# Weights converted in pairs of tiles, and the second layer's loads issued a step sooner

## The chip, the cores and the metric

The kernel runs on one core of a Trainium2 chip. The metric is the device time of one execution in microseconds (us), the median of several runs. TensorE multiplies matrices, VectorE and ScalarE work element by element, GpSimd (POOL) does some of the same, and SyncE (SP) issues most transfers; each engine works through its own instructions in program order.

## The reference, cut to what matters

```
x = attention(q, k, v)          # 4 batches x 576 tokens, 8 heads of 64, linear attention with decay
h = x @ w_in                    # 2304 tokens x 512 -> 2048
x = (h * sigmoid(h)) @ w_out    # first layer, 2048 -> 512
h = x @ w_in2
return (relu(h) ** 2) @ w_out2  # second layer, the same sizes
```

q, k and v are float32, the weights float64. The kernel reads a weight as a 64-bit word and turns it into float32 on the chip by integer steps. A product of two matrices is then made of a high part (rounded to the matmul's own format) and a low part (the rest): each product is high x high, high x low and low x high.

## The kernel before, in words

**Weights.** A tile is 128 x 512 words of 64 bits. Converting one takes four steps, each on one engine. `conv_a` (L107) makes two words of it with two activations on ScalarE (L115, L116). `conv_b` (L122 to L125) joins them on VectorE: a shift (L122), an addition (L123) and the sign (L125). `conv_c` casts the result to the high part on ScalarE (L137), and `conv_d` takes the difference, the low part, on VectorE (L141). `conv_to` runs the steps for tile i, i-1 and i-2 side by side. Raw tiles come by SP (`load_w`, L101) into a pool of three buffers (tag "wr"), the joined words into one of five (tag "wt"). There are 32 tiles in the first layer: wi (first GEMM) and wo (second GEMM) of 16 filters of 128 columns each.

**Blocks.** The first 1280 tokens of the first layer run in three blocks of 512, 384 and 384 tokens. Block 0 is where the weights are converted: for each filter f, `gemm1` (12 matmuls) makes ph, `gate` makes silu(ph) on ScalarE (L650) with its high part gh (L652), VectorE makes gl (L653), and two filters later `gemm2` (12 matmuls) adds to acc. The main loop (L1171) has two half-steps for each filter, and in each it emits conversions, waiting gates (`flush`), `gemm2` and attention. Attention for later tokens runs between the GEMMs as `scores_step` and `values_step`: `scores` (L369, L373) needs the keys scaled by `prep_k` (half of them on ScalarE, L358) and one PSUM tile, which `values` of the unit before it has to leave first; that unit's last reader is the difference xl (L465) on VectorE. `cut_consts(2)` (L306 to L309) cuts the tables that `prep_k` uses from then on, once, in the second half-step of the first filter.

**Second layer.** During block 1, the half-products of the other 1024 tokens (`product_s`) and their second GEMM (`gemm2_s`), `pre_step` walks a table of steps for the second layer's 16 pairs of tiles: load (`pre_load`), convert (`conv_a`, `conv_b`, one tile in each of two steps), four differences on GpSimd (`pre_sums`), and a store to DRAM. Behind it the second layer's products (L907, L998) run from DRAM copies. Transfers on SP are issued in program order, and one that waits for its buffer holds those behind it.

Of the kernel before, what the change touches and what calls it, by code (L numbers as in the profile page):

```python
# [29 lines left out]
LAG = 2  # L30
W1_FIRST, W1_AHEAD = 4, 4
AHEAD = 256
HALF = (slice(0, 64), slice(64, 128))
RAW = 3
# [9 lines left out]
def kernel(  # L44
# [23 lines left out]
    rp = l0_ctx.enter_context(tc.tile_pool(name="rp", bufs=RAW))  # L68
# [16 lines left out]

    wt = {}
    raw_w = {}
    order = sorted(range(2 * KF), key=lambda i: (i // 2 + i % 2 * LAG, i % 2))

    def w_at(n):  # L90

        layer, i = divmod(n, 2 * KF)
        return (layer, *divmod(order[i], 2))
# [25 lines left out]
    def conv_b(n, parts=(0, 1)):  # L119
        t, lo, hi = conv[n]  # L120
        if 0 in parts:
            nc.vector.tensor_scalar(t, t, 3, None, op0=ALU.logical_shift_left)  # L122
            nc.vector.tensor_tensor(t, t, lo, op=ALU.add)  # L123
        if 1 in parts:
            nc.vector.scalar_tensor_tensor(  # L125
                t, hi, -(2**31), t, op0=ALU.bitwise_and, op1=ALU.bitwise_or
            )

    def w_part(n):
        layer, f, part = w_at(n)  # L130
        if (part, f) not in wt:
            wt[part, f] = wp.tile([128, 2, 512], F32R, tag="w", name=("wi", "wo")[part])
        return wt[part, f][:, 0], wt[part, f][:, 1]
# [8 lines left out]

# [15 lines left out]
    woD = dp.tile([KF, 128, 2, 512], F32, name="woD")  # L158

    def keep_w(n):  # L160
        layer, f, part = w_at(n)
# [33 lines left out]
    def pre_parts(n):  # L195
        ta, tb = (conv["p", n, e][0].bitcast(F32) for e in range(2))
# [22 lines left out]
    def pre_store(n):  # L219
# [3 lines left out]
        if part == 0:  # L223
            nc.sync.dma_start(out=w1c[p, :, 0:512], in_=conv["p", n, 0][0].bitcast(F32))
# [8 lines left out]
        for e in range(2):  # L233
            conv.pop(("p", n, e))
# [4 lines left out]
    def pre_step():  # L239
# [37 lines left out]
    cs = cp.tile([128, 8 + 4 + 512 + 256 + 16], F32, name="cs")  # L277
    dummy = cp.tile([128, 1], F32, name="dummy")
    Tkn, dec = cs[:, 0:8], cs[:, 8:12]
# [31 lines left out]
    ap_ctx = ExitStack()  # L311
    ap = ap_ctx.enter_context(tc.tile_pool(name="ap", bufs=4, side="right"))
# [62 lines left out]
    def mask(u):  # L375
        rf_t[u] = rf = ap.tile([128, 2, 4, L], F32, tag="rf", name="rf", bufs=2)
# [176 lines left out]
    def first_units():  # L553
# [61 lines left out]
        conv_n[0] = 5  # L615
        conv_to(0, 6)
# [8 lines left out]
    def gemm1(layer, j, f, c0=0, c1=None):  # L625
# [6 lines left out]
        wh, wl = wt[0, f][:, 0], wt[0, f][:, 1]  # L632
# [12 lines left out]
    def gate(layer, j, f, ph):  # L645
# [3 lines left out]
        s = rp.tile([128, 512], F32, tag="wt", name="sg", bufs=5)[:, 0:n]  # L649
# [5 lines left out]
    def gemm2(layer, j, f):  # L655
        n = BLOCKS[j]
        gh, gl = g_t.pop((layer, j, f))
        wh, wl = wt[1, f][:, 0], wt[1, f][:, 1]
# [91 lines left out]
    def ws_at(p, c):  # L750
        if c in (0, 1, 6):
            w, c0 = wt[0, 2 * p + c // 6], c % 2 + c // 6
        else:
            w, c0 = ts[p, c // 2 - 1], c % 2
        return w[:, :, c0 * 256 : c0 * 256 + 256]

    def product_s(p, i):
# [5 lines left out]
        for k in range(2):  # L763
            w0 = slice(k * 128, k * 128 + 128)
            pairs += [(w[:, 0, w0], x[:, 0, k]), (w[:, 0, w0], x[:, 1, k]), (w[:, 1, w0], x[:, 0, k])]
# [666 lines left out]
```

## Time and profile before

| | |
|---|---|
| median of 3 runs | 828.31 us (828.2 to 828.74) |
| the profiled execution | 828.86 us, of which the span from the first to the last instruction is 827.1 us |
| TensorE busy | 811.1 us, 98% of the span |
| VectorE, ScalarE, GpSimd busy | 548.2, 450.5 and 184.3 us |
| mean granted TensorE clock | 0.998 |

An engine's busy time counts its instructions from start to end; TensorE's matmuls overlap, so its busy share says only that it has no gaps. A wait is a stretch in which an engine stands idle, put down to the instruction that released it.

### The profile page before, as it was taken

The page shows a single profiled execution, that of the slowest core. Times are in us where ns is not written, and L with a number is a line of the kernel's source. Part 1 is how long each engine was busy: PE and PEld are TensorE (multiplying, and loading weights), DVE is VectorE, ACT ScalarE, POOL GpSimd, SP SyncE. Part 2 cuts the span into 40 slices and gives each one's busy share as a digit, 9 for nine tenths or more (in the row PEclk, how much of TensorE's full clock was granted, in tenths as well). Part 3 has the DMA queues.
Part 4 walks back from the last instruction along what each step waited for, and adds up shares of the span by engine and source line. Part 5 has one row for each costly group of instructions (what it writes and reads, how often), then busy time and mean ns, then how long its engine had stood idle before and what let it go on. Part 6 is the DMA issues. An engine that isn't in the chain of part 4 may idle for free. (4 is left out here: it accounts for less than half of the span.)

```text
span 827.1 us, 16194 instructions
## 1 busy us (share of the span) xinstructions
PE 811.1 (98%) x6410; PEld 750.1 (91%) x6410; DVE 548.2 (66%) x809; ACT 450.5 (54%) x858; POOL 184.3 (22%) x205
## 2 busy tenths in 40 slices
PE   7999999999999999999999999999999999999998
PEld 6887789999888998888887999999999999999998
DVE  5799995554444655666778566545665988777771
ACT  5777874464455455454445576745667645433330
POOL 3202012313545204223432212401345000000000
PEclk9999999999999999999999999999999999999999
DMA  9787874987534022698787375243387844444300
GB/s 352 244 260 208 275 270 156 332 318 287 192 130 155 1 83 84 211 317 308 240 285 255 113 243 180 99 160 135 125 322 239 322 153 143 136 137 136 113 26 26
DMA packets 71980, 160.70 MB, mean 194 GB/s; under 512 B 6112, under 2 KB 37344, under 8 KB 71904
## 3 DMA queue, kind: packets, MB, share of 16 engines
q1 hardware_dynamic: 67008, 150.23, 53.5%
q10 hardware_dynamic: 4896, 9.44, 3.0%
q8 instruction: 50, 0.82, 0.4%
q14 instruction: 26, 0.21, 0.1%
HBM read 104.07 MB, written 55.57 MB: 193 GB/s over the span
## 5 line engine op out<-in xcount | busy, mean ns | idle before, releaser
L83 PE MATMUL acc<-gh,wo 128*128 128x384 f32 (+1 forms) x384 | 114.7, 360 | 0.0
L83 PE MATMUL ph<-xh,wi 128*128 128x384 f32 (+2 forms) x400 | 114.3, 350 | 0.0
L998 PE MATMUL pa<-w2s,gl 128*128 128x256 f32 x864 | 108.1, 283 | 0.0
L907 PE MATMUL pa<-xa,w1s 128*128 128x384 f32 x576 | 106.1, 335 | 0.7 <-DVE c L925 0.7
L998 PEld LDWEIGHTS pa<-w2s,gl 128*128 128x128 f32 x864 | 105.7, 192 | 0.0
L907 PEld LDWEIGHTS pa<-xa,w1s 128*128 128x128 f32 x576 | 100.3, 188 | 1.2 <-DVE c L925 1.0
L83 PE MATMUL acc<-gsl,wo 128*128 128x512 f32 x384 | 88.0, 390 | 0.5 <-DVE gsl L698 0.5
L83 PEld LDWEIGHTS acc<-gsl,wo 128*128 128x128 f32 x384 | 71.9, 188 | 16.4 <-DVE gsl L698 0.9
L697 ACT CAST gl<-gr 128x1024 fp32r<-128x1024 f32 (+1 forms) x57 | 55.7, 1002 | 51.8 <-DVE gr L972 25.3
L998 PE MATMUL pb<-w2s,gl 128*128 128x256 f32 x648 | 82.0, 283 | 0.0
L907 PE MATMUL pb<-xa,w1s 128*128 128x384 f32 x432 | 81.1, 336 | 0.0
L998 PEld LDWEIGHTS pb<-w2s,gl 128*128 128x128 f32 x648 | 79.6, 192 | 0.0
L83 PEld LDWEIGHTS ph<-xh,wi 128*128 128x128 f32 x400 | 72.7, 188 | 5.4
L83 PEld LDWEIGHTS acc<-gh,wo 128*128 128x128 f32 x384 | 71.5, 190 | 6.1
L907 PEld LDWEIGHTS pb<-xa,w1s 128*128 128x128 f32 x432 | 75.5, 188 | 0.5 <-DVE u L919 0.5
L698 DVE TENSOR_TENSOR gl<-gr,gl 128x1024 fp32r<-128x1024 f32 (+1 forms) x55 | 64.5, 1180 | 8.0 <-ACT gl L697 8.0
L83 PE MATMUL ph<-xl,wi 128*128 128x384 f32 (+2 forms) x200 | 69.3, 346 | 0.0
L83 PE MATMUL acc<-gl,wo 128*128 128x384 f32 (+1 forms) x192 | 68.6, 357 | 0.0
L653 DVE TENSOR_TENSOR gl<-sg,gh 128x384 fp32r<-128x384 f32 (+1 forms) x48 | 30.8, 643 | 47.6 <-ACT gh L652 47.6
L115 ACT ACTIVATE t<-wr 128x512 f32<-128x512 f32 x64 | 43.1, 673 | 28.3 <-DMA wr<-w 24.5
L650 ACT ACTIVATE sg<-ph 128x384 f32<-128x384 f32 (+1 forms) x48 | 25.0, 522 | 56.7 <-PE ph L83 54.5
L123 DVE CUSTOM_DVE_ANT_0 t<-wr,t 128x1024 uint16<-128x1024 uint16 x64 | 46.8, 731 | 7.7
(144 smaller groups left out, 1338.0 us busy)
## 6 DMA issues: line engine op xcount, KB each, us to landing
wr<-w SPq DMA_DIRECT2D x64, 512.0 KB, 4.4
gD<-g SPq DMA_DIRECT2D x48, 384.0 KB, 2.7
gr<-gD SPq DMA_DIRECT2D x36, 512.0 KB, 4.8
raw<-att SPq DMA_DIRECT2D x32, 512.0 KB, 4.6
woD<-wo SPq DMA_DIRECT2D x16, 512.0 KB, 7.1
wo<-woD SPq DMA_DIRECT2D x16, 512.0 KB, 7.4
w2r<-w2c SPq DMA_DIRECT2D x14, 512.0 KB, 6.1
xq<-x SPq DMA_DIRECT2D x12, 384.0 KB, 5.9
```

Of the source, the lines that this page charges most:

```text
L83: mm(o, a, b, start=first and i == 0, stop=last and i == n - 1)
L115: nc.scalar.activation(t.bitcast(F32), hi.bitcast(F32), ACTF.Abs, scale=2.0**-112)
L123: nc.vector.tensor_tensor(t, t, lo, op=ALU.add)
L650: nc.scalar.activation(s, ph, ACTF.Silu)
L653: later.append(lambda: nc.vector.tensor_sub(gl, s, gh))
L697: nc.scalar.copy(dst[0], src)
L698: low.append(lambda: engine.tensor_sub(dst[1], src, dst[0]))
L907: mm(o, lhs, rhs, start=m == 0 and i in (0, 1, 4), stop=m == 5, skip_group_check=True)
L998: mm(o, lhs, rhs, start=first, stop=m == NP - 1 and q == 2, skip_group_check=True)
```

## The change

Six tiles of the first layer (`SINGLES`) are converted as before, from buffers of the weight pool. The other 26 go in 13 pairs: two neighbouring filters of wi or of wo. The shift, the cast and the difference of a pair are single instructions over 1024 columns; the words, the addition and the sign are one instruction per raw tile, or one for the pair where both tiles came by one load into a single 8 KB buffer (tag "r8": three pairs of wi and the last of wo). `conv_step` puts the steps of a pair into half-steps: the words of pair q (`pair_a`) and the addition and sign of pair q-1 in one, the cast of pair q-1, its difference (behind the gates) and the shift of pair q in the next. In the first two half-steps it also finishes tiles 4 and 5. In the second layer each pair is loaded by one transfer into the "r8" buffer, one step sooner than before, its words made in one step and joined in the next. Buffers are laid out anew: the tables move to attention's pool, the mask has one buffer, the gates' tile a tag of its own with two, and the temporaries of the last stage always come from their pool. The saved wo goes to DRAM by pair and part. `pre_step` runs from the thirteenth product on and once per filter in the second GEMM of the half-products.

```diff
-W1_FIRST, W1_AHEAD = 4, 4
+W1_FIRST, SINGLES = 4, 6
 AHEAD = 256
 HALF = (slice(0, 64), slice(64, 128))
-RAW = 3
 WARM = 5
 NP = KF // 2
 HB = 384
...
+    w_order = [divmod(i, 2) for i in order[:SINGLES]]
+    pairs = [(part, j + 2 - part) for j in range(NP) for part in range(2) if j + 2 - part < NP]
+    def tiles_of(part, j):
+        if (part, j) not in w_pair:
+            w_pair[part, j] = ab = [
+                wp.tile([128, 2, 512], F32R, tag="w", name=("wi", "wo")[part] + nm) for nm in "hl"
+            ]
+            for e in range(2):
+                wt[part, 2 * j + e] = (ab[0][:, e], ab[1][:, e])
+        return w_pair[part, j]
     def load_w(n):
-        layer, f, part = w_at(n)
-        if n < W1_FIRST:
+        if n < SINGLES:
+            f, part = w_order[n]
             r = wp.tile([128, 512], U64, tag="w", name="wr")
-        else:
-            r = rp.tile([128, 512], U64, tag="wr", name="wr")
-        nc.sync.dma_start(out=r, in_=(w1, w2)[layer][f, part])
-        raw_w[n] = r
+            nc.sync.dma_start(out=r, in_=w1[f, part])
+            raw_w[n] = r
+            return
+        part, j = pairs[n - SINGLES]
+        if (part == 0 and j % 2 == 0) or (part and j == NP - 1):
+            r = rp.tile([128, 1024], U64, tag="r8", name="wr", bufs=1)
+            src = w1[2 * j : 2 * j + 2, part].rearrange("f p n -> p f n")
+            nc.sync.dma_start(out=r.rearrange("p (f n) -> p f n", f=2), in_=src)
+            raw_w[n] = [r]
+        else:
+            raw_w[n] = [wp.tile([128, 512], U64, tag="w", name="wr") for _ in range(2)]
+            for e, r in enumerate(raw_w[n]):
+                nc.sync.dma_start(out=r, in_=w1[2 * j + e, part])
     conv = {}
     first = {}
-    def conv_a(n):
-        r = raw_w.pop(n).bitcast(I32).rearrange("p (n t) -> p n t", t=2)
-        lo, hi = r[:, :, 0], r[:, :, 1]
-        if n in range(W1_FIRST):
-            t = wp.tile([128, 512], I32, tag="w", name="t")
-            first[n] = t
-        else:
-            t = rp.tile([128, 512], I32, tag="wt", name="t", bufs=5)
+    def words(r):
+        r = r.bitcast(I32).rearrange("p (n t) -> p n t", t=2)
+        return r[:, :, 0], r[:, :, 1]
+    def to_words(t, lo, hi):
         nc.scalar.activation(t.bitcast(F32), hi.bitcast(F32), ACTF.Abs, scale=2.0**-112)
         nc.scalar.activation(lo, lo.bitcast(U32), ACTF.Copy, scale=2.0**-29)
+    def add_sign(t, hi):
+        nc.vector.scalar_tensor_tensor(t, hi, -(2**31), t, op0=ALU.bitwise_and, op1=ALU.bitwise_or)
+    def conv_a(n):
+        lo, hi = words(raw_w.pop(n))
+        t = first[n] = wp.tile([128, 512], I32, tag="w", name="t")
+        to_words(t, lo, hi)
         conv[n] = (t, lo, hi)
...
+    def pair_a(n):
+        part, j = pairs[n - SINGLES] if isinstance(n, int) else (0, 0)
+        pool, tag = (wp, "w") if part and j < NP - 2 else (rp, "wr")
+        t = pool.tile([128, 1024], I32, tag=tag, name="t")
+        pieces = []
+        raws = raw_w.pop(n)
+        for e, r in enumerate(raws):
+            cols = 1024 // len(raws)
+            pieces.append((t[:, e * cols : e * cols + cols], *words(r)))
+            to_words(*pieces[-1])
+        conv[n] = (t, pieces)
+    def pair_b(n, part):
+        t, pieces = conv[n]
+        if part == 0:
+            nc.vector.tensor_scalar(t, t, 3, None, op0=ALU.logical_shift_left)
+        for tp, lo, hi in pieces:
+            if part == 1:
+                nc.vector.tensor_tensor(tp, tp, lo, op=ALU.add)
+            elif part == 2:
+                add_sign(tp, hi)
+    def pair_c(n):
+        nc.scalar.copy(flat(tiles_of(*pairs[n - SINGLES])[0]), conv[n][0].bitcast(F32))
+    def pair_d(n):
+        a, b = tiles_of(*pairs[n - SINGLES])
+        nc.vector.tensor_sub(flat(b), conv.pop(n)[0].bitcast(F32), flat(a))
...
     def keep_w(n):
-        layer, f, part = w_at(n)
+        if n < SINGLES:
+            f, part = w_order[n]
+            dst, t = w1f[f // 2, :, f % 2], first.pop(n)
+        else:
+            part, j = pairs[n - SINGLES]
+            dst, t = w1f[j].rearrange("p e n -> p (e n)"), conv[n][0]
         if part == 0:
-            t = first.pop(n) if n in first else conv[n][0]
-            nc.sync.dma_start(out=w1f[f // 2, :, f % 2], in_=t.bitcast(F32))
-    n_loaded = [0]
-    load_end = [2 * KF]
-    conv_n = [0, 0]
-    def load_next():
-        if n_loaded[0] < load_end[0]:
-            load_w(n_loaded[0])
-            n_loaded[0] += 1
-    def conv_to(layer, n):
-        for i in range(conv_n[layer], min(n, 2 * KF + 2)):
-            conv_n[layer] += 1
-            for lag, stage in ((2, conv_c), (0, conv_a), (1, conv_b), (2, conv_d)):
-                if 0 <= i - lag < 2 * KF:
-                    stage(layer * 2 * KF + i - lag)
-                    if stage is conv_b and n_loaded[0] < i - lag + layer * 2 * KF + RAW + 1:
-                        load_next()
-                    if stage is conv_b:
-                        keep_w(i - lag)
+            nc.sync.dma_start(out=dst, in_=t.bitcast(F32))
+    def conv_step(n):
+        if n < 2:
+            if n == 0:
+                conv_b(5)
+                load_w(SINGLES + 1)
+            conv_c(4 + n)
+            conv_d(4 + n)
+            if n == 0:
+                keep_w(4)
+                return
+        q, odd = divmod(n - 1, 2)
+        q += SINGLES
+        first, end = SINGLES, SINGLES + len(pairs)
+        if odd:
+            if first < q <= end:
+                pair_c(q - 1)
+                behind.append(lambda: pair_d(q - 1))
+            if q < end:
+                pair_b(q, 0)
+            return
+        if q < end:
+            pair_a(q)
+        if q + 2 < end:
+            load_w(q + 2)
+        if first < q <= end:
+            pair_b(q - 1, 1)
+            pair_b(q - 1, 2)
+            keep_w(q - 1)
...
     def pre_load(n):
         part, p = divmod(n, NP)
-        for e in range(2):
-            r = rp.tile([128, 512], U64, tag="wr", name="wr")
-            nc.sync.dma_start(out=r, in_=w2[2 * p + e, part])
-            raw_w["p", n, e] = r
+        r = rp.tile([128, 1024], U64, tag="r8", name="wr", bufs=1)
+        src = w2[2 * p : 2 * p + 2, part].rearrange("f p n -> p f n")
+        nc.sync.dma_start(out=r.rearrange("p (f n) -> p f n", f=2), in_=src)
+        raw_w["p", n] = [r]
...
-            if k == 0:
+            if k == (-1 if n else 0):
                 pre_load(n)
             elif k == 2:
-                conv_a(("p", n, 0))
+                pass
             elif k == 3:
-                conv_b(("p", n, 0))
-                conv_a(("p", n, 1))
+                pair_a(("p", n))
             elif k == 4:
-                conv_b(("p", n, 1))
+                for part in range(3):
+                    pair_b(("p", n), part)
...
         conv_a(4)
-        conv_n[0] = 5
-        conv_to(0, 6)
+        conv_c(3)
+        conv_a(5)
+        conv_b(4)
+        conv_d(3)
...
-        s = rp.tile([128, 512], F32, tag="wt", name="sg", bufs=5)[:, 0:n]
+        s = rp.tile([128, 512], F32, tag="sg", name="sg", bufs=2)[:, 0:n]
...
-                    conv_to(0, 2 * f + half + 1 + W1_AHEAD)
+                    conv_step(2 * f + odd)
...
-        if n >= 16 and n % 2 == 0:
+        if n >= 12 and n % 2 == 0:
             pre_step()
...
-        for _ in range(1 + n % 2 * (n < KF)):
-            pre_step()
+        pre_step()
```

## Rows read from the trace of the kernel before

**Rows 1.** The page: busy time, and VectorE and the granted clock in 40 slices of the span.

```profile
PE 811.1 (98%) x6410; PEld 750.1 (91%) x6410; DVE 548.2 (66%) x809; ACT 450.5 (54%) x858; POOL 184.3 (22%) x205
...
DVE  5799995554444655666778566545665988777771
...
PEclk9999999999999999999999999999999999999999
```

**Rows 2.** Windows by stage: stretch, us, each engine's busy us, clock, DMA share, GB/s.

```profile
60.00:100.00 40.00, 37.58 (x332) 30.26 (x331) 37.77 (x65) 30.74 (x57) 4.23 (x5) 0.96 0.81 250
```

**Rows 3.** Waits of TensorE: us in total, times, longest.

```profile
PE P L369 <- DVE xl L465: 2.4, 2, 2.0
...
PE P L369 <- ACT raw L358: 1.4, 3, 0.7
```

**Rows 4.** Timeline of VectorE: start, us, line, operation; start-up and two tiles of block 0.

```profile
31.56 0.69 DVE L125 SCALAR_TENSOR_TENSOR t<-wr,t 128x512 int32<-128x512 int32 x1
...
81.45 0.42 DVE L122 TENSOR_SCALAR t<-t 128x512 int32<-128x512 int32 x1
81.99 0.69 DVE L123 CUSTOM_DVE_ANT_0 t<-wr,t 128x1024 uint16<-128x1024 uint16 x1
82.72 0.69 DVE L125 SCALAR_TENSOR_TENSOR t<-wr,t 128x512 int32<-128x512 int32 x1
83.33 0.69 DVE L141 TENSOR_TENSOR wi<-t,wi 128x512 fp32r<-128x512 f32 x1
83.93 0.42 DVE L122 TENSOR_SCALAR t<-t 128x512 int32<-128x512 int32 x1
...
87.01 0.42 DVE L122 TENSOR_SCALAR t<-t 128x512 int32<-128x512 int32 x1
```

**Rows 5.** Timeline of TensorE in block 0; in brackets the idle time before.

```profile
38.37 0.50 PE L83 MATMUL acc<-gh,wo 128*128 128x512 f32 x1
...
53.43 0.39 PE L83 MATMUL ph<-xh,wi 128*128 128x512 f32 x1
...
58.87 0.39 PE L83 MATMUL ph<-xh,wi 128*128 128x512 f32 x1
...
94.67 0.69 PE L369 MATMUL P<-raw 64*64 64x64 f32 x32 [2.03 <-DVE xl L465]
...
95.77 0.68 PE L83 MATMUL acc<-gh,wo 128*128 128x512 f32 x1
...
100.22 0.39 PE L83 MATMUL ph<-xh,wi 128*128 128x512 f32 x1
```

**Rows 6.** Windows behind the stop at 94.67; the clock stands behind GpSimd's busy time.

```profile
96.00:97.00 1.00, 1.00 (x3) 0.82 (x3) 1.00 (x3) 0.97 (x3) 0.00 (x0) 0.50 0.76 285
```

**Rows 7.** Timeline of TensorE in the second GEMM of the half-products.

```profile
441.11 5.05 PE L83 MATMUL acc<-gsl,wo 128*128 128x512 f32 x21 [0.47 <-DVE gsl L698]
```

**Rows 8.** Groups by shape: count, busy us, mean ns of one, idle before.

```profile
L698 DVE TENSOR_TENSOR gl<-gr,gl 128x1024 fp32r<-128x1024 f32 x51 | 61.9, 1219 | 8.0 <-ACT gl L697 8.0
L697 ACT CAST gl<-gr 128x1024 fp32r<-128x1024 f32 x51 | 52.3, 1048 | 51.8 <-DVE gr L972 25.3 <-PE pa L998 12.2 <-DVE gr L974 9.8
...
L697 ACT CAST gl<-gr 128x512 fp32r<-128x512 f32 x6 | 3.4, 615 | 0.0
...
L698 DVE TENSOR_TENSOR gl<-gr,gl 128x512 fp32r<-128x512 f32 x4 | 2.6, 685 | 0.0
```

**Rows 9.** Timeline of ScalarE at the start of block 0.

```profile
36.54 1.05 ACT L358 ACTIVATE raw<-raw,cs 128x64 f32<-128x64 f32 x4
37.50 0.60 ACT L137 CAST wi<-t 128x512 fp32r<-128x512 f32 x1
38.01 0.67 ACT L115 ACTIVATE t<-wr 128x512 f32<-128x512 f32 x1
38.58 0.66 ACT L116 ACTIVATE wr<-wr 128x512 int32<-128x512 uint32 x1
```

**Rows 10.** The page's transfers: count, size, median us from issue to landing.

```profile
wr<-w SPq DMA_DIRECT2D x64, 512.0 KB, 4.4
```

More of the change, by code (lines that the diff above doesn't have):

```diff
@@ L86 @@
     wt = {}
+    w_pair = {}
     raw_w = {}
     order = sorted(range(2 * KF), key=lambda i: (i // 2 + i % 2 * LAG, i % 2))
-    def w_at(n):
-        layer, i = divmod(n, 2 * KF)
-        return (layer, *divmod(order[i], 2))
+    w_order = [divmod(i, 2) for i in order[:SINGLES]]
[8 more added lines that the diff above has]
+        return w_pair[part, j]
@@ L124, in conv_b @@
         if 1 in parts:
-            nc.vector.scalar_tensor_tensor(
-                t, hi, -(2**31), t, op0=ALU.bitwise_and, op1=ALU.bitwise_or
-            )
+            add_sign(t, hi)
     def w_part(n):
-        layer, f, part = w_at(n)
-        if (part, f) not in wt:
-            wt[part, f] = wp.tile([128, 2, 512], F32R, tag="w", name=("wi", "wo")[part])
-        return wt[part, f][:, 0], wt[part, f][:, 1]
+        f, part = w_order[n]
+        tiles_of(part, f // 2)
+        return wt[part, f]
     def conv_c(n):
@@ L195, in pre_parts @@
     def pre_parts(n):
-        ta, tb = (conv["p", n, e][0].bitcast(F32) for e in range(2))
+        t = conv["p", n][0].bitcast(F32)
+        ta, tb = t[:, 0:512], t[:, 512:1024]
         b11, b12, b21, b22 = ta[:, 0:256], tb[:, 0:256], ta[:, 256:512], tb[:, 256:512]
@@ L232, in pre_store @@
             nc.sync.dma_start(out=w2c[6, :, cols], in_=b22)
-        for e in range(2):
-            conv.pop(("p", n, e))
+        conv.pop(("p", n))
     pre_at = [5 * n if n < 6 else 3 + 5 * n for n in range(2 * NP)]
@@ L275 @@
     FOUR = ((0, 0), (1, 1), (0, 1), (1, 0))
-    cs = cp.tile([128, 8 + 4 + 512 + 256 + 16], F32, name="cs")
     dummy = cp.tile([128, 1], F32, name="dummy")
+    ap_ctx = ExitStack()
+    ap = ap_ctx.enter_context(tc.tile_pool(name="ap", bufs=4, side="right"))
+    cs = ap.tile([128, 8 + 4 + 512 + 256 + 16], F32, tag="cs", name="cs", bufs=1)
     Tkn, dec = cs[:, 0:8], cs[:, 8:12]
@@ L375, in mask @@
     def mask(u):
-        rf_t[u] = rf = ap.tile([128, 2, 4, L], F32, tag="rf", name="rf", bufs=2)
+        rf_t[u] = rf = ap.tile([128, 2, 4, L], F32, tag="rf", name="rf", bufs=1)
         nc.vector.tensor_mul(rf, P_of[u][:, :, 0:256].rearrange("p e (a t) -> p e a t", a=4), Tm)
@@ L753, in ws_at @@
         else:
-            w, c0 = ts[p, c // 2 - 1], c % 2
-        return w[:, :, c0 * 256 : c0 * 256 + 256]
+            w, c0 = (ts[p, c // 2 - 1][:, e] for e in range(2)), c % 2
+        return [part[:, c0 * 256 : c0 * 256 + 256] for part in w]
     def product_s(p, i):
@@ L764, in product_s @@
             w0 = slice(k * 128, k * 128 + 128)
[L765 removed]
+            pairs += [(w[0][:, w0], x[:, 0, k]), (w[0][:, w0], x[:, 1, k]), (w[1][:, w0], x[:, 0, k])]
         for m, (lhs, rhs) in enumerate(pairs):
@@ L800, in load_wo @@
         wo[f] = t = wp.tile([128, 2, 512], F32R, tag="w", name="wo")
-        nc.sync.dma_start(out=t.bitcast(F32), in_=woD[f])
+        src = woD[f // 2, :, :, f % 2].rearrange("e p n -> p e n")
+        nc.sync.dma_start(out=t.bitcast(F32), in_=src)
     acc_s = {}
@@ L1000, with temp2 @@
     outs = []
-    def temp2(P, nm):
-        if P % 2:
-            return pools["tq"].tile([128, 256], F32, tag=nm, name=nm, bufs=1)
-        c0 = 12 + 256 * ("s1", "u2", "u3").index(nm)
-        return cs[:, c0 : c0 + 256]
+    def temp2(nm):
+        return pools["tq"].tile([128, 256], F32, tag=nm, name=nm, bufs=2)
     def after2(P, i):
@@ L1090 @@
             nc.sync.dma_start(out=raw[0][g][:, a:b], in_=att[g, :, a:b])
-    load_next()
+    load_w(0)
     for g in range(NG):
         nc.sync.dma_start(out=raw[0][g][:, 256:768], in_=att[g, :, 256:768])
-    load_next()
+    load_w(1)
     load(1)
     load(2)
-    load_next()
+    load_w(2)
     load(3)
-    while n_loaded[0] < W1_FIRST:
-        load_next()
-    for n in range(RAW):
-        load_next()
+    for n in range(3, SINGLES + 1):
+        load_w(n)
     first_units()
@@ L1185 @@
                 prep_k(n_start)
-        for half in range(2):
-            if i == 0 and half:
+        for odd in range(2):
+            if i == 0 and odd:
                 cut_consts(2)
-            step = 2 * (i - (nb - 1) * KF) + half
+            step = 2 * (i - (nb - 1) * KF) + odd
             if step >= 0:
@@ L1193 @@
                 if j == 0:
-                    conv_to(0, 2 * f + half + 1 + W1_AHEAD)
+                    conv_step(2 * f + odd)
                 if j == 1 or step == 0:
                     pre_step()
-                if j == 1 and half == 0:
-                    nc.sync.dma_start(out=woD[f], in_=wt[1, f].bitcast(F32))
+                if j == 1 and odd == 0:
+                    nc.sync.dma_start(out=woD[f // 2, f % 2], in_=w_pair[1, f // 2][f % 2].bitcast(F32))
                 if j == nb - 1:
@@ L1205 @@
                 flush()
-            if half and i >= LAG:
+            if odd and i >= LAG:
                 gemm2(*seq[i - LAG])
@@ L1209 @@
                 a0, a1 = att_end(j), att_end(j + 1)
-                run_att(a0 + (a1 - a0) * (2 * f + half + 1) // (27, 29, 22)[j])
+                run_att(a0 + (a1 - a0) * (2 * f + odd + 1) // (27, 29, 22)[j])
     flush()
```

20 lines of the change are left out of this document (10 added, 10 removed).

## The prediction

> **What bounds the kernel now.** I read the page's busy line first: TensorE works 98% of the span, and in the row of slices VectorE reaches nine tenths only in the third to sixth, 41 to 124 us [rows 1]. So an edit is worth only the TensorE stops that it removes, less those that it makes. TensorE's list of waits [rows 3] gives the stops. In reach of the change are "P <- DVE xl" (2.4 us in two) and one of the three "P <- ACT raw".
>
> Block 0 is where the first layer's weights are converted, and there VectorE is busy 37.77 of 40 us [rows 2]. One tile takes it from the shift at 81.45 to the next at 83.93, 2.48 us; two tiles and a gate's difference reach from 81.45 to 87.01, 5.56 us. TensorE asks for this every 5.44 us (58.87 - 53.43). So VectorE falls behind, attention's work comes on top [rows 4, 5]. TensorE's scores wait for its xl (L465): 2.03 us before 94.67, and the rest of the 2.4, 0.40, in an earlier unit. The second stop costs more than itself. The granted clock is 0.50, the 1.2 GHz level, between 96 and 97 us [rows 6], and the twelve matmuls from 95.77 to 100.22 take 4.45 us instead of half of 5.44, 2.72: 1.73 us more [rows 5]. VectorE's lateness thus costs 0.40 + 2.03 + 1.73 = 4.16 us, plus 0.47 us at 441 us [rows 7], where a gate's difference comes late behind conversions.
>
> **The change part by part.** *VectorE's price of a pair.* Two tiles take 2 x 2.48 = 4.96 us now. In a pair the shift becomes one 1024-wide instruction: between 0.54 (as now for one) and 1.08 us (twice), I take 0.8, because TENSOR_TENSOR of 1024 columns costs 1.78 times one of 512 (1219 to 685 ns) [rows 8]. The add no longer stands right behind its shift, so I take 0.61 us (the spacing of the sign step) instead of 0.73: 1.22 for two; the signs stay 1.22. One 1024-wide difference costs 1219 ns, less the overlap of 0.09, 1.13 instead of 1.21. Sum 4.4, bounds 4.1 and 5.0. Saved per pair 0.56 (0 to 0.86), over 13 pairs 7.3 us of VectorE. With the gate's 0.6 us, VectorE needs 5.0 us where TensorE needs 5.44: it no longer sets the pace, and xl, some 10 pairs into the block, comes 5 us sooner, where 2.03 would do. So I take all of 4.16 as removed; the other bound is 0.40.
>
> *The order on ScalarE at the block's start.* This is the new cost. Today the calls of the first steps convert nothing: the constants are cut up to 36.54, then L358 scales unit 4's keys (36.54, four instructions, about 1.05 us), and only then come the next cast and words at 37.50 [rows 9]. TensorE's scores of unit 4 stand right behind these keys (one of the three waits for ACT raw [rows 3]), and the first product of the second GEMM follows at 38.37 [rows 5]. In the changed kernel step 0 casts tile 4 ahead of the gates, and step 1 puts the cast of tile 5 and the words of the first pair, two activations of 1024 columns, between the constants and the keys. Program order is kept on this engine, so all of it stands in front of TensorE. Working: tile 4's signs end at 31.56 + 0.69 = 32.25 [rows 4], its cast takes 0.53 of issue spacing, the first gate starts at about 32.78; the second gate waited for TensorE before, so its end, and the constants with it, slip 0.45 only. The cast of tile 5 adds 0.53 (37.50 to about 38.03). Words of 512 columns are 0.57 apart (38.01 to 38.58); 512 columns more cost 1048 - 615 = 0.43 [rows 8], so 1.0 each, 2.0 for two. Sum 0.45 + 0.53 + 2.0 = 2.98 us later keys, hence about 2.95 us of a new stop. Its bounds are 2.1 (words no dearer than for 512) and 3.3 us (twice 512), if the first pair's load has landed; it is issued right behind the singles at the start, so I take that it has. Behind the waiting scores stand all further matmuls; nothing covers it.
>
> *The clock behind that stop.* TensorE does almost nothing from 36.7 to about 40.6 us, longer than before 94.67, where the clock fell. No row shows a stop in this place: below, nothing; above, 1.73, the price that the row shows, or about 3.5 if it stays down twice as long. Part of the slow stretch can fall into the scores' slow issue, so I take 1.1.
> The Trainium skill, "TensorE: Matmul & The Clock Gate", Part 1, says that the lower clock is the default and that recent activity releases it, so that an idle array goes back to half rate. The fall to 0.50 behind the 94.67 stop agrees; by the rule alone the new stop would be paid with the full 1.73 and the forecast would be 0.6 us later.
>
> *Loads and slots in block 0.* A pair is loaded two pairs ahead, four half-steps of 2.72 us, against a median landing of 4.4 us for one tile [rows 10]. Merged loads go to a single 8 KB buffer, used by every fourth pair. The load of the next user is issued after the words of the last were read, so neither SP nor the attention loads queued behind it should stand long. The words' lead over the cast also costs nothing: each pair's cast comes 1.5 to 2 filters ahead of its first matmul, 8 to 11 us, and cast and difference need about 2.3.
>
> *The second layer.* Its 16 pairs save VectorE again some 0.5 us each, but stand where VectorE has room [rows 1]; so nothing comes of it but the 0.47 us at 441 [rows 7], because the loads no longer share buffers with stores that must land first. Against it: the three VectorE steps of a pair now stand in one call, about 3.1 us in one piece (estimate from the 1024-wide rows [rows 8]; 1.8 to 3.6) instead of two of 1.9. In the half-products this stands in front of the additions that free PSUM. A product of six matmuls lasts a quarter of 5.44, 1.36 us, and a bank is written again four products later, so 5.4 us of cover hold 3.1 + 2 additions of 0.7 (as the 512-wide difference [rows 8]). In the stage behind it the split is needed two filters later, again 5.4 us. Cost nothing; if the cover is gone, about 0.5 us for each of four to eight places. The tables' move to another pool, the mask's single buffer (scores of the next unit follow the values of this one on TensorE anyway), the temporaries of the last stage and the woD layout with 2 KB runs are off the path: 0.
>
> **Sum.** -4.16 - 0.47 + 2.95 + 1.1 = -0.6 us. The profiled execution took 828.86 (span 827.1 and 1.76 around it), the median of the runs is 828.31, 0.55 below; from the median I forecast 827.8.
>
> **The rivals.** First, *the early stop is cheap*: the clock holds there, or the first words are shorter than worked out. Then -4.63 + 2.95 = -1.7 gives 826.6, and with the stop at its lower bound of 2.1, 825.8. For it: the clock shows no fall in the page's slices of the start-up, which has gaps too [rows 1]. Against: the stop is longer than the one at 94.67. It counts as faster from 826.65 down.
>
> Second, *the clock takes the gain*: at the new stop, at 37 to 41 us, the 1.2 GHz level costs twice what it did behind 94.67. It decides from a price of 3.35 us on: -4.63 + 2.95 + 3.5 = +1.8, 830.1. The rule cited above is its ground, and the longer idle stretch speaks for it; that the clock came back behind 94.67 after twelve matmuls speaks against.
>
> Third, *the pairs are not quicker on VectorE*: at the upper bound of 5.0 per pair it stays behind and the 2.03 and 1.73 remain: 828.31 + 2.95 + 1.1 - 0.9 = 831.5. The 1024-wide rows speak against it.
>
> Fourth, *the long piece* in the half-products stops TensorE at four places: -0.6 + 2 = 829.7, still no measurable change.
>
> **How the numbers follow.** Forecast (and the fourth) 0.50, first rival 0.28, second 0.12, third 0.10. Measurable from no change is about 0.2%, 1.66 us: below 826.65 or above 829.97. The first rival alone ends faster; the second and third slower. So faster 0.28, same 0.50, slower 0.22. The likeliest case's own range is 826.7 to 829.7; to leave out no more than 2 in 10 the range reaches into the first rival and to the second: 825.6 to 830.2.
>
> **What would show it.** Right: the wait "P <- ACT raw L358" grown to about 3 us with two 1024-wide words in front of the keys; no wait for xl beyond 0.5 us; VectorE under 36 of 40 us between 60 and 100; clock 0.50 somewhere in 39 to 45 and 1.00 around 96; no gap at 441. Wrong: keys scaled before the pair's words, the stop at 94 still there, or new waits of TensorE for u, gs or gsl in the second half.

## The result, and the profile after

The change made the kernel slower: 839.08 us (median of 4 runs, 838.43 to 840.04) against 828.25 us, a ratio of 1.0131 (95% interval 1.0114 to 1.0149), where 827.8 was forecast. The profiled execution took 838.43 us, its span is 836.6. In this part and the next, lines such as L973 are those of the changed kernel.

First comes the page of the changed kernel: its busy line and three of its rows of slices.

```profile
PE 814.0 (97%) x6410; PEld 752.1 (90%) x6410; DVE 539.0 (64%) x727; ACT 441.8 (53%) x805; POOL 186.3 (22%) x205
...
PE   7899999999999999999999799999999999999998
...
DVE  5799963554344667564679567645666988777772
...
PEclk9999999999999999999999899999999999999999
```

VectorE worked 9.2 us less than in [rows 1] and ScalarE less too, yet the span grew by 9.5 us. TensorE has a dip that was not there, in the slice from 460 to 481 us, and the clock has one in the same slice. The list of TensorE's waits in the changed kernel names the places (us in total, times, longest).

```profile
PE pa L973 <- ACT s L981: 4.7, 1, 4.7
PE P L432 <- ACT raw L421: 4.0, 3, 2.9
...
PE pa L832 <- DVE gs L852: 1.0, 1, 1.0
PE acc L82 <- DVE gsl L763: 1.0, 1, 1.0
```

Against [rows 3], the waits for xl are gone, the wait for ScalarE's keys is the one forecast, and three others are new or larger. To see what each costs, I set the times at which TensorE reaches the same work side by side, from its timeline in both profiled executions:

| TensorE reaches | before | after | lost in the stage |
|---|---|---|---|
| the first acc | 38.37 | 41.66 | 3.3 |
| the last acc of the first layer's blocks | 299.83 | 300.30 | -2.8 |
| the first product of the second layer (L907, now L973) | 465.50 | 467.86 | 1.9 |
| the last GEMM's first matmul (L998, now L1064) | 641.95 | 651.40 | 7.1 |
| the end of the span | 827.1 | 836.6 | 0.1 |

The last column is the growth of the delay since the row above. So block 0, which the argument was about, came out nearly even, and most of the loss lies where the prediction wrote 0.

**The start.** Timeline of ScalarE, then of TensorE, in the changed kernel (start, duration, engine, line, operation; in brackets the idle time before it and what ended it). The last line is TensorE's wait for the same keys in the kernel before.

```profile
37.02 0.20 ACT L374 ACTIVATE cs<-cr 128x4 f32<-128x4 f32 x1
37.13 0.60 ACT L157 CAST woh<-t 128x512 fp32r<-128x512 f32 x1
37.64 1.13 ACT L130 ACTIVATE t<-wr 128x1024 f32<-128x1024 f32 x1
38.67 1.13 ACT L131 ACTIVATE wr<-wr 128x1024 int32<-128x1024 uint32 x1
39.69 1.05 ACT L421 ACTIVATE raw<-raw,cs 128x64 f32<-128x64 f32 x4
```

```profile
36.93 0.45 PE L432 MATMUL P<-raw 64*64 64x64 f32 x8 [0.34 <-POOL raw L418]
40.32 0.75 PE L432 MATMUL P<-raw 64*64 64x64 f32 x6 [2.94 <-ACT raw L421]
...
41.66 0.79 PE L82 MATMUL acc<-gh,woh 128*128 128x512 f32 x1
42.25 0.63 PE L82 MATMUL acc<-gl,woh 128*128 128x512 f32 x1
...
45.93 0.39 PE L82 MATMUL ph<-xh,wih 128*128 128x512 f32 x1
```

```profile
37.16 0.75 PE L369 MATMUL P<-raw 64*64 64x64 f32 x6 [0.37 <-ACT raw L358]
```

The cast of tile 5 and the two 1024-wide activations stand between the constants and the keys, as worked out from [rows 9], and TensorE waits 2.94 us where it waited 0.37. Behind it the matmuls take 0.63 us in place of 0.39: the granted clock is 0.50, the 1.2 GHz level, from 42 to 44 us. The twelve from 41.66 to 45.93 take 4.27 us, 1.55 more than half of 5.44 [rows 5]. In the kernel before, the same twelve took 2.88 us (38.37 to 41.25), so against it the clock cost 1.39.

**VectorE in block 0.** Timeline of VectorE in the changed kernel, one pair and one gate's difference.

```profile
79.31 0.68 DVE L181 TENSOR_SCALAR t<-t 128x1024 int32<-128x1024 int32 x1
79.91 1.22 DVE L193 TENSOR_TENSOR wil<-t,wih 128x1024 fp32r<-128x1024 f32 x1
81.04 1.28 DVE L184 CUSTOM_DVE_ANT_0 t<-wr,t 128x1024 uint16<-128x1024 uint16 x2
82.25 1.28 DVE L134 SCALAR_TENSOR_TENSOR t<-wr,t 128x512 int32<-128x512 int32 x2
83.45 0.68 DVE L718 TENSOR_TENSOR gl<-sg,gh 128x512 fp32r<-128x512 f32 x1
84.05 0.68 DVE L181 TENSOR_SCALAR t<-t 128x1024 int32<-128x1024 int32 x1
```

From shift to shift it is 4.74 us, where [rows 4] showed 5.56 for the same work. The windows of the changed kernel show that this did not make VectorE idle: the columns are the window, its length, busy time and count of PE, PEld, DVE, ACT and POOL, the granted clock, the DMA share and GB/s.

```profile
60.00:100.00 40.00, 40.00 (x351) 32.76 (x350) 38.41 (x54) 33.24 (x55) 6.56 (x8) 1.00 0.69 253
92.00:100.00 8.00, 8.00 (x95) 6.46 (x95) 7.02 (x12) 7.06 (x12) 1.53 (x3) 1.00 0.36 125
```

38.41 of 40 us stands against 37.77 in [rows 2]: what was saved is filled with attention's operations. But TensorE has no gap in the window and the clock is 1.00 where it was 0.50 [rows 6].

**The stop at 477 us.** TensorE's timeline at the start of the second layer in the changed kernel, then ScalarE's, then two lines of its DMA view for 464 to 470 us (count, size of one, median us from issue to landing).

```profile
467.86 2.24 PE L973 MATMUL pa<-xa,w1s 128*128 128x384 f32 x12
469.94 2.25 PE L973 MATMUL pb<-xa,w1s 128*128 128x384 f32 x12
476.91 4.21 PE L973 MATMUL pa<-xa,w1s 128*128 128x384 f32 x12 [4.72 <-ACT s L981]
480.91 2.59 PE L973 MATMUL pb<-xa,w1s 128*128 128x384 f32 x12
483.34 2.24 PE L973 MATMUL pa<-xa,w1s 128*128 128x384 f32 x12
```

```profile
468.68 0.33 ACTq L890 DMA_DIRECT2D x<-y  x1
469.05 0.62 ACT L762 CAST w1s<-w1r 128x512 fp32r<-128x512 f32 x1 [0.40 <-ACT y L888]
476.37 0.48 ACT L981 COPY s<-pa 128x384 f32<-128x384 f32 x1 [6.71 <-DMA x<-y]
```

```profile
x<-y SPq DMA_DIRECT2D x2, 256.0 KB, 6.5
x<-y ACTq DMA_DIRECT2D x2, 256.0 KB, 7.3
```

TensorE waits for a PSUM bank that ScalarE has to copy into the tile s, and ScalarE waits 6.71 us for a transfer that has nothing to do with s: the first layer's result y, on its way to DRAM. Such a wait suggests that s and y lie on the same memory. The sizes in the code agree. The conversion pool "rp" grew from 3 x 4,096 + 5 x 2,048 = 22,528 to 8,192 + 2 x 2,048 + 3 x 4,096 = 24,576 bytes of a partition, with its "wr" buffers, one of which holds y, now last. The second layer opens its pools on the same place: gq (18,432), cq (4,608), then tp, where s lies. tp thus starts at 23,040: behind the old pool's end, but inside the last buffer of the new one. Behind the stop, two chains take 6.43 us (476.91 to 483.34) in place of 2 x 2.08, at a granted clock of 0.60 and 0.55 in the two windows of 4 us from 474 to 482. The stop of 4.72 and this 2.27 make 7.0 of the 7.1 us.

**The long piece.** VectorE's timeline in the half-products of the changed kernel.

```profile
370.10 1.23 DVE L763 TENSOR_TENSOR gsl<-gs,gsl 128x1024 fp32r<-128x1024 f32 x1 [1.50 <-ACT gsl L762]
371.25 0.68 DVE L843 TENSOR_TENSOR u<-pb,s 128x512 f32<-128x512 f32 x1
371.85 0.68 DVE L181 TENSOR_SCALAR t<-t 128x1024 int32<-128x1024 int32 x1
372.56 1.23 DVE L184 CUSTOM_DVE_ANT_0 t<-wr,t 128x2048 uint16<-128x2048 uint16 x1
373.82 1.22 DVE L134 SCALAR_TENSOR_TENSOR t<-wr,t 128x1024 int32<-128x1024 int32 x1
374.97 1.28 DVE L852 TENSOR_TENSOR gs<-pa,u 128x512 f32<-128x512 f32 x2
```

A second-layer pair holds VectorE for 3.1 us in one piece, the addition gs comes behind it, and TensorE's next product stops 1.01 us for it at 375.70. In the second GEMM the stop for gsl before 448.49 is 0.95 us, twice that of [rows 7].

### The profile page after: what moved, and what is told of

It reads as the page before. It is cut to its first block, busy times and chain, and to the rows that moved or that the text cites. A ratio compares the mean times of both kernels' runs of the same rounds, so it can differ in the third digit from the quotient of the medians.

```text
span 836.6 us, 15936 instructions
## 1 busy us (share of the span) xinstructions
PE 814.0 (97%) x6410; PEld 752.1 (90%) x6410; DVE 539.0 (64%) x727; ACT 441.8 (53%) x805; POOL 186.3 (22%) x205
## 4 chain that ended last, share of the span: by engine, by line
PE 77%; DMA 6%; POOL 3%; issue 3%; DVE 3%; ACT 3%; SPq 1%; POOLq 0%; ACTq 0%; DVEq 0%
PE acc L82 15%; PE pa L1064 12%; PE pa L973 12%; PE ph L82 10%; PE pb L1064 9%; PE pb L973 9%; PE pa L832 5%; PE pb L832 3%; DMA w2c<-t 2%; PE Q L482 1%; DVE t L184 1%; DMA wr<-w 1%; DMA x<-y 1%; POOL raw L448 1%; DVE t L134 1%
## 5 line engine op out<-in xcount | busy, mean ns | idle before, releaser
L973 PE MATMUL pa<-xa,w1s 128*128 128x384 f32 x576 | 108.1, 340 | 5.4 <-ACT s L981 4.7
L1064 PE MATMUL pa<-w2s,gl 128*128 128x256 f32 x864 | 108.1, 283 | 0.0
L973 PEld LDWEIGHTS pa<-xa,w1s 128*128 128x128 f32 x576 | 102.0, 191 | 6.3 <-ACT s L981 5.0
L1064 PEld LDWEIGHTS pa<-w2s,gl 128*128 128x128 f32 x864 | 105.7, 192 | 0.0
L1064 PE MATMUL pb<-w2s,gl 128*128 128x256 f32 x648 | 82.0, 283 | 0.0
L973 PE MATMUL pb<-xa,w1s 128*128 128x384 f32 x432 | 81.5, 337 | 0.0
L1064 PEld LDWEIGHTS pb<-w2s,gl 128*128 128x128 f32 x648 | 79.6, 192 | 0.0
L973 PEld LDWEIGHTS pb<-xa,w1s 128*128 128x128 f32 x432 | 76.0, 189 | 0.4 <-DVE u L985 0.4
L82 PE MATMUL ph<-xh,wih 128*128 128x384 f32 (+2 forms) x200 | 70.8, 354 | 0.0
L82 PE MATMUL acc<-gh,woh 128*128 128x384 f32 (+1 forms) x192 | 70.0, 365 | 0.0
L82 PE MATMUL ph<-xl,wih 128*128 128x384 f32 (+2 forms) x200 | 69.4, 347 | 0.1
L82 PE MATMUL ph<-xh,wil 128*128 128x384 f32 (+2 forms) x200 | 69.2, 346 | 0.0
L82 PE MATMUL acc<-gh,wol 128*128 128x384 f32 (+1 forms) x192 | 68.3, 356 | 0.0
L82 PE MATMUL acc<-gl,woh 128*128 128x384 f32 (+1 forms) x192 | 68.2, 355 | 0.0
L130 ACT ACTIVATE t<-wr 128x512 f32<-128x512 f32 (+1 forms) x44 | 38.7, 880 | 22.7 <-DMA wr<-w 22.7
L985 DVE TENSOR_TENSOR u<-pb,s 128x384 f32<-128x384 f32 x48 | 26.0, 554 | 31.7 <-PE pb L973 30.7
```

What stands on the lines that cost most here:

```text
L82: mm(o, a, b, start=first and i == 0, stop=last and i == n - 1)
L973: mm(o, lhs, rhs, start=m == 0 and i in (0, 1, 4), stop=m == 5, skip_group_check=True)
L985: nc.vector.tensor_add(st[nm], o, st["s1"])
L1064: mm(o, lhs, rhs, start=first, stop=m == NP - 1 and q == 2, skip_group_check=True)
```

## The experiments

Theory 1 is the ledger above: separate stops, each with a cause of its own. The kernel before was run beside each group; its medians there were 828.4 to 828.7, and ratios are against it. The changed kernel was not run again, so a difference from it, or between groups, is uncertain by some 0.4 us more.

**1. The shared memory.** The second layer's pools are opened with tp first, so that s comes to lie elsewhere; in the changed kernel, and in the one before.

```diff
-    for name, bufs in (("gq", 6), ("cq", 1), ("tp", 1)):
+    for name, bufs in (("tp", 1), ("cq", 1), ("gq", 6)):
```

> The changed kernel with one edit: the small pool of the second layer's first products (s, u) is opened ahead of the other two, so that it lies on buffers whose last reader ends at 458 us. Theory 1 (shared memory): the conversion pool has grown by 2 KB, so the first buffer of s lies on one that still holds the half-products' result y until its transfer lands; ScalarE's first copy waits for that. Then the 4.72 us stop of TensorE at 472 goes, with the 2.4 us of half clock behind it: about 832.0. Theory 2 (late conversions): the thinner pace of the second layer's steps fills the queues and engines at that place, whatever the memory; then no change, 839 and a stop of 4 to 5 us.

Measured: 831.89 us, ratio 1.0035 (1.0022 to 1.0048), 7.2 less than the change, as theory 1 expected. TensorE's timeline at the same place of this kernel:

```profile
469.73 2.24 PE L973 MATMUL pb<-xa,w1s 128*128 128x384 f32 x12
471.81 2.24 PE L973 MATMUL pa<-xa,w1s 128*128 128x384 f32 x12
```

The products run on without a gap. One line in the order of three pools carries two thirds of the loss; the shared memory is the cause. That the 2,048 bytes brought it about is worked out from the sizes; no run changes the size alone.

> The kernel before with the same edit, which here puts s and u onto the buffers of y (in the kernel before they lie 512 bytes beyond them). Theory 1: ScalarE's first copy of s now waits for y's transfer in the kernel before too, and TensorE stops for 0.5 to 3 us at about 470, less than in the changed kernel since y lands sooner there (3.5 us after issue, not 7): 829 to 833. Theory 2: no change, 828.3.

Measured: 829.21 us, 1.0008 (0.9998 to 1.0018), and no stop at the products: the one that theory 1 expected here did not come. So the order by itself neither costs nor gains. It does not show what a shared buffer would cost in the kernel before: s then lies on the first of three "wr" buffers, y needs two of them, and ScalarE's copy of s starts at 467.15 without a wait.

**2. Why y is late.** The last pair's stores were issued at 443 to 444 us before, now at 463 to 464, right ahead of the tables' loads and of y (SP's timeline, the last store before and after):

```profile
443.52 0.50 SPq L232 DMA_DIRECT2D w2c<-t  x1
463.50 0.50 SPq L296 DMA_DIRECT2D w2c<-t  x1
```

The reason is the pace: the second layer's steps in the half-products and their GEMM number 54 where they were 60. Two experiments end the conversions sooner. The first takes back the old pace:

```diff
-        if n >= 12 and n % 2 == 0:
+        if n >= 16 and n % 2 == 0:
...
-        pre_step()
+        for _ in range(1 + n % 2 * (n < KF)):
+            pre_step()
```

> The changed kernel with the second layer's steps at the pace of before (from product 16 on, and three in two filters in the first half of the second GEMM), so that its last stores go out some 16 us sooner. Theory 1: the wait for y stays but ends when y lands, 3.5 instead of 7 us after issue: the stop shrinks to 0.5 to 2 us, 833 to 836. Theory 2: it goes wholly, 832.

Measured: 849.32 us, 1.0251 (1.0236 to 1.0266). The stop for s shrank to 1.78 us, but new ones of 5.80, 1.82 and 3.22 us stand at 407.5, 410.1 and 458.6, and from 408 to 416 the clock is again 0.50. ScalarE's timeline of this kernel shows why:

```profile
404.81 1.12 ACT L130 ACTIVATE t<-wr 128x1024 f32<-128x1024 f32 x1 [13.45 <-POOL wt L280]
...
406.87 1.64 ACT L762 CAST gsl<-gs 128x512 fp32r<-128x512 f32 x3
```

The words of a pair wait 13.45 us for a "wr" buffer that GpSimd's sums still use, and three casts that TensorE needs stand behind them. The sums had themselves stood idle 16.58 us for a store out of such a buffer. The change's buffers do not bear the old pace. The second experiment doubles only four steps, late in the GEMM:

```diff
-        pre_step()
+        for _ in range(1 + (n in (11, 15, 19, 23))):
+            pre_step()
```

> The changed kernel, its pools as they are, with four further conversion steps in the second GEMM of the half-products (at its steps 11, 15, 19 and 23), so that the last weight pair is finished four steps, some 11 us, sooner. In the changed kernel its last stores are issued at 463 to 464 us, just ahead of the loads of the tables and of the results y (466.8), and y lands 6.5 to 7.3 us after its issue; in the kernel before they were issued at 443 to 444, and y landed after 2.2 to 3.5. Theory 2 (the stop of 4.72 us needs both the shared memory and the late end of the conversions, which puts stores and table loads in front of y): the last stores go out by about 453, y lands in 2 to 4 us, the stop for ACT s shrinks to 0.5 to 2 us and the slow clock behind it mostly goes; 832 to 835.5. Rival (shared memory alone sets the stop, y is as late as ever): 4 us or more remain, 838 to 840.

Measured: 838.98 us, 1.0119 (1.0105 to 1.0133). The total is the rival's, the mechanism is theory 2's. Waits of TensorE in this kernel, then two lines of its DMA view for 468 to 475 us:

```profile
PE acc L82 <- DVE gsl L763: 5.0, 4, 1.7
...
PE pa L973 <- ACT s L981: 1.8, 1, 1.8
```

```profile
x<-y SPq DMA_DIRECT2D x2, 256.0 KB, 2.3
x<-y ACTq DMA_DIRECT2D x2, 256.0 KB, 3.4
```

y lands in 2.3 and 3.4 us, the stop for s is 1.79 in place of 4.72 and the chains behind it take 2.35 us, at a clock of 1.00, with a stop of 0.74 for u between them. But each doubled step holds the words of a pair and its three operations on VectorE, in front of a split that TensorE waits for: four stops for gsl, 5.0 us in all. So the stop for s needs the shared memory, and about 2.9 us of its length come from the late end.

**3. The start.** In the changed kernel the keys (and the next attention load) are issued right behind the constants:

```diff
             if i == 0 and odd:
                 cut_consts(2)
+                prep_k(n_start)
+                load(n_start + 1)
...
-            if i == 1:
-                load(n_start + 1)
-                prep_k(n_start)
```

> The changed kernel with unit 4's keys scaled right behind the cut constants, ahead of tile 5's cast and the first pair's words. If the prediction's step on ScalarE's order holds, the 2.94 us stop at 37 us shrinks to about 0.8 (the keys still come 0.5 us later than in the kernel before) and the 1.2 GHz stretch behind it (12 matmuls in 4.37 instead of 2.72 us) goes: 3.5 to 4.0 us less, about 835. Rival: the pair's words, now later, hold the first pair's difference and a new stop for wi appears: no gain.

Measured: 836.66 us, 1.0099 (1.0084 to 1.0114), 2.4 less where 3.5 to 4.0 were expected. The stop for the keys is 0.37 us; in its place TensorE stops 1.15 us at 40.73 for gl, which VectorE reaches only behind tile 5's difference, and matmuls of 0.63 us follow. This timeline of VectorE in the same kernel shows the order:

```profile
38.84 0.69 DVE L161 TENSOR_TENSOR wol<-t,woh 128x512 fp32r<-128x512 f32 x1 [3.26 <-ACT woh L157]
39.45 2.36 DVE L718 TENSOR_TENSOR gl<-sg,gh 128x512 fp32r<-128x512 f32 x2
```

Of the 2.8 us between the two profiled executions, 1.4 are the stop for s, here 3.34. That the two repairs do not simply add was seen when they were put together.

> The change with two repairs: the second layer's pools in the order of the tables first, and the keys of block 0's last unit issued right behind the constants. Theory 1 (the 10.8 us are separate stops, each with its own cause and its own price): the two repairs add up. The first alone gave 831.89 (839.08 before it, 7.2 less), the second alone 836.66 (2.4 less), so both give 829.5 (829.0 to 830.0), and the stop of 1.15 us of the first accumulation for VectorE's gl stays. Rival (a stop removed early only turns up later, because something behind TensorE sets the end): 831.5 or more, and the second half of the span takes longer than with the pools alone.

Measured: 830.67 us, 1.0022 (1.0013 to 1.0030), between both theories' bounds: the keys are worth 1.2 us once the pools are apart. Then tile 5's difference goes behind the gates':

```diff
-            conv_d(4 + n)
...
+            behind.append(lambda: conv_d(5))
```

> As the one before, and besides the difference of weight tile 5 is issued behind the first gates' differences on VectorE instead of ahead of them. Theory 1 (the remaining stop at 40.73 us and the slow clock behind it, 7 matmuls of 0.63 us in place of 0.39, come from the gates' differences that wait behind that tile's): the stop of 1.15 us goes, the clock holds, 1.2 to 2.5 us less than with the two repairs: 827.0 to 828.3. Rival (the pause of the engine before, the keys' stop of 0.37 us and the small score matmuls, is enough for the slow clock): the stop goes but matmuls of 0.63 us stay, 828.3 to 829.0.

Measured: 829.07 us, 1.0005 (0.9996 to 1.0013). The gain of 1.6 is theory 1's; the total lies just above the rival's range, since both started from a total 1.2 too low. No stop is left at 38 to 42 us, the clock is 1.00 from 38 to 46, and the last acc of the first layer comes at 297.31, 2.5 us sooner than before the change.

**4. The long piece.** The pair's sign goes one step later, in the changed kernel with its pools reordered:

```diff
-                for part in range(3):
-                    pair_b(("p", n), part)
+                pair_b(("p", n), 0)
+                pair_b(("p", n), 1)
             elif k in (5, 6):
+                if k == 5:
+                    pair_b(("p", n), 2)
```

> The change with the pools reordered, and the second layer's pair operations split over two steps: the sign goes one step later. Theory 1 (the stops of 1.02 us at 375.51 for gs and 0.96 us at 448.29 for gsl come from the three pair operations of 3.1 us in one step on VectorE): the gs stop shrinks to 0 to 0.3 us, half-products and their second GEMM take 1 to 2 us less together, 830.0 to 831.0. Rival (the stops come from what else stands ahead on VectorE in those steps, the second block's token splits of 1.5 us): both stops stay, 831.5 to 832.3.

Measured: 831.55 us, 1.0032 (1.0018 to 1.0046), 0.3 less than with the pools alone: the rival's total. Yet both stops are gone from TensorE's list, and from the last acc of the first layer to the second layer's first product it takes 165.25 us in place of 167.54. The products then take 177.7 us in place of 176.4 up to the last GEMM, so that 1.0 us remains in the profiles, which the interval of the medians does not exclude. TensorE's timeline of this kernel at the products:

```profile
475.60 2.35 PE L975 MATMUL pb<-xa,w1s 128*128 128x384 f32 x12 [0.73 <-DVE u L987]
```

With the sign a step later, the store of the last pair's sums goes out at 465.71 in place of 462.84, and lands after 3.6 us; ScalarE's copy of y, which takes over such a buffer, starts at 469.48 in place of 466.53: what was gained ahead meets the late end of the conversions, as in the next experiment.

**5. All together.**

> All four repairs together: pools in the other order, keys behind the constants, tile 5's difference behind the gates', sign a step later. Theory 1 (separate stops): the sum, 831.9 less 2.4, less 1.2 to 2.5, less 0.5 to 1.9: 825.5 to 827.8, under the kernel before by 0.4 to 2.7 us. Rival (VectorE's pair pieces hold something up in any order): 828 to 830, no faster than the kernel before.

Measured: 828.87 us, 1.0009 (0.9996 to 1.0022): the rival's total again. The second layer's products start at 462.86, 2.0 us sooner than with the first three repairs (group 3), but two stops stand there in this kernel's timeline:

```profile
467.77 2.36 PE L976 MATMUL pa<-xa,w1s 128*128 128x384 f32 x12 [0.59 <-ACT s L984]
470.87 2.35 PE L976 MATMUL pb<-xa,w1s 128*128 128x384 f32 x12 [0.73 <-DVE u L988]
```

The last pair's stores go out up to 462.7 us, and y lands after 5.5 and 6.3 us. By the times, ScalarE's copy of y in this kernel waits for the store of the last sums, whose buffer it takes over, issued at 460.44 and landed after 4.0 us; the profile names a product of TensorE that has nothing to do with y:

```profile
464.60 0.59 ACT L891 COPY y<-acc 128x512 f32<-128x512 f32 x1 [7.95 <-PE pa L976]
```

The casts and the copies of s stand behind it on ScalarE. The question is whether that lateness or the order of casts makes the stops. Three kernels ask it: the four repairs with the four doubled steps of experiment 2, three of them (without the split sign) with the same, and

```diff
-    pre_at = [5 * n if n < 6 else 3 + 5 * n for n in range(2 * NP)]
+    pre_at = [5 * n for n in range(2 * NP)]
```

the four repairs with the conversions ended three steps sooner by leaving out a pause.

> The four repairs and the four further steps. With the four repairs alone the second GEMM ended 2 us sooner, but stops of 0.59 us (ACT s) and 0.73 us (DVE u) came at the first products of the second layer, and the median was 828.87. Theory 2 (they come from the last pair's stores, issued up to 462.7, whose buffers y takes over): both stops go, 826.0 to 827.8, faster than the kernel before by 0.5 to 2.5 us. Rival (they come from the tables' casts on ScalarE, which have the same place in the order whatever the stores do): 828.3 to 829.3 again.

Measured: 830.47 us, 1.0020 (1.0010 to 1.0029). Both stops went, so they came from the lateness, but the doubled steps made three for gsl, 2.5 us; neither total was right. The copy of y on ScalarE starts 1.1 us ahead of the first product here; with the four repairs alone it was 1.7 behind it.

> Pools in the other order, keys sooner, tile 5's difference behind the gates', and the four further steps, but the three pair operations of a second-layer pair in one step, as in the change. Theory 2 (the one-piece VectorE work costs about 2 us in two stops, gs 1.0 and gsl 1.0 us, whatever the pace): both stops stay, 828.3 to 829.5, some 2 us above the run with the sign a step later. Rival (they go away with the pace, because they stem from where the steps fall): 826 to 828.

Measured: 833.58 us, 1.0050 (1.0037 to 1.0063). The stop for gs stayed at 1.0 us, as theory 2 had it, those for gsl grew to four with 5.0 us, and the total is 4 us above its range. The pieces of VectorE work in front of the splits are what TensorE pays for: 5.0 us where a pair's three operations are in one step, 2.5 with the sign apart, at the same pace.

> The four repairs, and the second layer's conversions end three steps (some 8 us) sooner without doubling any step: the pause of three steps that the schedule makes ahead of its seventh pair is left out. Theory 2: y's buffers and the SP queue are free when the second GEMM ends, so the stops of 0.59 (ACT s) and 0.73 us (DVE u) at the start of the second layer go; no step holds two pairs' work, so no stop for gsl above 0.5 us as in the runs with doubled steps. 826.3 to 828.0, faster than the kernel before by 0.6 to 2.3 us. Rival (the pause was needed: without it the seventh pair's steps fall among the table transforms that end the first layer, on VectorE and in the same buffers): new stops of over 1 us between 290 and 330 us, 828.5 to 831.

Measured: 826.88 us, 0.9986 (0.9971 to 1.0000). The stops for s and u at the first products are gone, and the only one for gsl is 0.3 us, as theory 2 had it; no stop of over 1 us stands between 290 and 330 us. It has the lowest median of all kernels here, 1.5 us under the one before, but the interval just reaches no change, so that it is faster than the kernel before is not shown. Its executions spread from 825.36 to 831.7; the profiled one, 831.7, has a stop of 2.0 us for xh in the first layer that no other profile has in this size; its cause stays open.

## Why the prediction was wrong

- **"Nothing comes of it" for the second layer, with the new layout of buffers "off the path: 0", failed by some 7 us.** The step looked at who uses each buffer while its pool is open, and not at what comes to lie on its memory afterwards. The tables' move, which the prediction names there, is not what did it: they left another pool. The new tags "r8" and "sg" made "rp" 2,048 bytes larger and put "wr" last in it, and so s lies on a buffer that a transfer still reads. Experiment 1 shows the shared memory, the sizes in the code the rest.
- **The pace of the conversions had no term in the sum.** With 54 steps in place of 60 the last stores go out 20 us later, and that lengthens the stop for s from 1.8 to 4.7 us (experiment 2). **And the 0.47 us at 441** did not go but doubled. It was put down to loads that share buffers with stores; both stops of 1.0 us went when VectorE's work was spread (experiment 4), with the loads as they were.
- **"Cost nothing" for the one-piece pair failed, by about 2 us.** The fourth rival had the mechanism, with four places of 0.5 us; it was two of 1.0 (experiments 4 and 5). The cover of 5.4 us was reckoned as if VectorE were free when the piece begins; in the timeline a split and an addition of 1.9 us stand right ahead of it.
- **The early stop was nearly right, in mechanism and size.** The keys come 3.15 us later (39.69 against 36.54) where 2.98 was worked out, behind just the instructions named. That 2.95 meets the measured 2.94 so closely is partly luck: the forecast was of a new stop, and 0.37 of the 2.94 stood there before, so 2.57 is new.
- **The clock behind it** was mis-sized: 1.1 forecast; measured 1.55 over the full clock, or 1.39 over the kernel before. Which of 1.1 and the upper price of 1.73 came nearer depends on which of the two one takes. The stop of 4.72 us at 477 cost 2.27, the dearest; but as 2.03 had cost 1.73 and 2.94 costs 1.55, length alone does not set the price, and the second rival's 3.5 was not seen.
- **VectorE's price of a pair was nearly right:** a pair and a gate take 4.74 us, 5.0 forecast. **"VectorE under 36 of 40 us" was wrong** (38.41) without harm: all that mattered was that xl came in time. Of the 4.16 us, about 4.2 came back: 3.3 us behind at the first acc and 1.39 more lost to the clock, TensorE is only 0.5 us behind at the end of the first layer's blocks.
- By the sum's own terms: the first layer -0.1 (measured 0.5), the half-products and their GEMM -0.5 (1.9), the second layer 0 (7.1). (The terms add to -0.58, which from 828.31 gives 827.7 and not 827.8; nothing hangs on it.) The first two rivals argued over some 2 us at the start, while most of the loss lay at a place that no rival named.

The Trainium skill, "SBUF — State Buffer", "The DMA setup-cost knee", fits a transfer's time as 2 us and its bytes over 436 GB/s. For y's 256 KB that is an estimate of 2.6 us; 2.3 and 3.4 us with the four doubled steps lie around it; 6.5 and 7.3 in the changed kernel do not. There SP issues two of the tables' loads from 464.12 on, just ahead of y at 466.80, and two more from 468.51. A transfer that holds a buffer must be priced in its company.

## What to carry to other kernels

When a pool changes its size, list the pools that open on its place later and what may still be reading there; a wait for a transfer that has nothing to do with the tile is the sign of it. Merging small operations saves the engine time, but what counts is the longest piece in front of an operation that TensorE waits for. And count the steps of a background schedule to its end: if it ends later, its stores meet the next stage's loads.

## What the runs showed that I had not expected

A stop of the same length did not always bring the clock down: behind 1.15 us at 40.7 us the matmuls took 0.63 us with the keys alone moved, while behind 1.14 us at 40.5, with the pools reordered too, the granted clock stayed at 1.00 from 38 to 46 us. The two kernels differ only in the order of pools that are opened behind 460 us, so this looks like a difference between executions; its cause stays open. The stops of 1.4 to 1.8 us with the four doubled steps were also followed by matmuls at full speed: 48 in 11.17 us.
